# A written-out order for sigmoid attention with a token mixer: another order, eight casts on VectorE, no held transfers

## The chip, the cores and the metric

The kernel runs on one core of a Trainium2 chip. The metric is the device time of one execution in microseconds. A core has five engines with queues of their own, each worked off strictly in order: TensorE (PE; its weight loads are shown as PEld), VectorE (DVE), ScalarE (ACT), GpSimd (POOL) and SyncE (SP), which issues the transfers between HBM and the on-chip memory. A matmul writes to one of eight accumulator banks (PSUM), and VectorE or ScalarE has to copy it out before the bank is used again.

## The reference

For 8 batches, 12 heads, 448 tokens and a head size of 64, attention with a sigmoid in place of the softmax, and a token mixer on its output:

```python
scores = scale * np.matmul(q, k.transpose(0, 1, 3, 2)) - np.log(S)
attn = 1.0 / (1.0 + np.exp(-scores))
x = np.matmul(attn, v)                  # heads side by side: (8, 448, 768)
...
W_tok = scale * np.einsum('bsd,btd->bst', x @ w_q, x @ w_k)
mixed = np.einsum('bst,btd->bsd', W_tok, x)
out = np.maximum(mixed, 0.0) @ w_out
```

Inputs and output are float32. There is no normalisation in either part, so the mixer is reassociated: the kernel forms the 64 x 768 matrix of keys times x first, and multiplies the queries by it.

## The kernel before

**Units of work.** Four heads of a batch are a *quad*; there are 24 quads, three to a batch. A quad's scores come in seven pieces (168 in all). A piece is four 64 x 64 matmuls with 448 columns that run side by side on the four quarters of the array and fill a pair of banks; one sigmoid on ScalarE reads the pair and writes bf16 (line 332). Four more quarter-array matmuls multiply the piece with the values (`values`), and after seven pieces VectorE copies the quad's output to the tile `xt` (line 356).

**Steps of the mixer.** When a batch's three quads are there, the kernel transposes x (`tr_x`, copied out in line 385), projects it (`mlp_wqk`), transposes the keys, forms `tmp`, mixes (`mlp_mix`, relu in line 468 or 470) and multiplies by `w_out` (`out_chunk`, `out_pair`; copies in lines 604 and 651, stores in 612 and 657).

**Two tilings of the array.** Attention, `tmp` and the mix use quarters of the array (64*64 in the profile). The projection, the output product of the first four batches, and a part of the x transposes use the whole array (128*128). Every step from the one kind to the other is a change of tiling; there are 84 in the program. A few steps use 128*64.

**How q and k get into place.** q, k and v of a quad are loaded as float32 into a ring of six buffers (`ld`), cast to bf16 (line 212 for most q and k, line 222 for v and the first quads), and q and k are then turned so that the head dimension lies along the partitions. There are two ways for the later quads. Kind `c`: GpSimd swaps quadrants of the cast tile (`arrange`: one copy in line 167, two in 170, two in 173), and VectorE finishes with two 32 x 32 block transposes (line 272). Kind `r`: nothing on GpSimd, and VectorE makes six transposes (two in line 265, four in 252). The cast tiles have two buffers, so the casts for a quad wait until VectorE has read those of the quad two before.

**What sets the order.** Nothing is scheduled by a tool. `PLAN` is a string with one letter for each step: S a piece of scores with its sigmoid, T a piece of scores whose sigmoid is left to the next S, so that one ACTIVATE reads both, P and p a values product, q k the first quads' transposes, c and d the two transposes of a quad of kind `c`, r s z those of kind `r`, x y X Y the x transposes (capital: on the whole array), W w L l, N, U u, M m, O o the mixer's steps, D a store, C a copy of `w_out` to the other half of the partitions, E and F matmuls on zeros that keep TensorE busy at the start, 1 the next cast that VectorE does. Small letters of P, W, U, M and O put the copy out on ScalarE. `BANKS` gives each step its bank or pair of banks. `ORDER` is the order of loads and casts; an entry with a point in front is cast by VectorE, the others by GpSimd. A load is issued when the cast that frees its buffer has been written in the program. `BEHIND` makes two late loads wait for a given matmul, and `HELD` three stores.

Of the kernel before, what the change touches and what calls it, by code (L numbers as in the profile page):

```python
# [17 lines left out]
def kernel(  # L18
# [29 lines left out]
    def pool(name, bufs, **kw):  # L48
# [15 lines left out]
    pairs = [banks[:, 2 * n : 2 * n + 2] for n in range(4)]  # L64
    pairs16 = [banks16[:, 2 * n : 2 * n + 2] for n in range(4)]
    BANKS = (
        "abcd0123200233111020302312031203101031021g2012020120h1g21320"
        "132123103103213012302g01h20h1g2031a32102312g12h1201321gh0210"
        "12h01210321g201321g2h01gh201g20132cd302c302302131e301230ef31"
        "0ef3102102c302d320d320123cd20gh120g102310g102hg102312gh10210"  # L70
        "ef130210ef1302120120320312321031021021321a310320321320120123"
        "020210320120c3210210312"
    )
    given = list("".join(BANKS))
    held = set()
# [54 lines left out]
    def xt(u, j):  # L130
# [5 lines left out]


    PLAN = (
        "SSFKESSES1EEqESDD1DESjPPppSpDpPDSSSqS1kSpPPSqSpSkSDPPSPSxSxr"
        "sSWwDDDDSSwzDPpSPppSpPSrSwSwWsSPpXSPNpSpPPSUSqSzMSSkpSpPpSMS"  # L140
        "ppPSSxSxMScPpSdPSpppSSPwWwrWSSXWDWSSosOSNPpPSpppzPSSOOSxSrPP"
        "ppSUSsppzPSoSOSoSoSppMpSPPPPSSWOWWWScSdxWODSMDWSOSxCOSMppScP"
        "DppSPPDSodDoSpxPDPDSCPrPSpDSPOOSNSsSOoDzOOSUSXcSPdpPSSpPPSPo"
        "OWSMSwowWMSSOwWCScpppSxpdpSpPSOoMSPPcDSPPpSpSPOoNSSSdDOoDOOp"
        "xDSPpPxSPpPDSuwcWwdSSMWOoSMSDwwOOSDxpPSPrPSmPpPDooNDSDSosoOz"
        "oSDDSxOOSUDpSDPPPDSPpcDSPoDODSSSodOoOSPMpSPPPSPPSwWwoScMSdOw"
        "wSSWOONSPMPcpSPPPPSSOodXSOSxoSoxSOppSpcUPSPpPSoOSdSxOOSPPPmp"
        "pPSPoSoMmOSOLScllLSLLSDodODSONxOPSpcpdpDPSPSPoOSoSOSOoSUSoSO"
        "SpPPpp1SoSOpSPOSOyppPMpPpplMlmlxlLlxOoONooUoOMmooOmooOoOOOOO"
        "oOOOOooOo"  # L150
    )
    PLAN = "".join(PLAN)
    KIND = ["a"] + [t for t in PLAN if t in "qacr"]
# [364 lines left out]

    opened = []
    stores, o_tiles = [], [0]  # L520
    HELD = {(5, 1, 1): 3040, (5, 2, 0): 3168, (5, 2, 1): 3168}

    def flush(n=None):

# [45 lines left out]
    def out_pair(act, tail):  # L570
# [36 lines left out]
        def store():  # L607
            for x in range(2):
                cols = slice(x * NB, (x + 1) * NB)
                if len(us) == 1:  # L610
                    behind_product(
                        (nc.scalar if ends and x else nc.sync).dma_start(
                            out=out[2 * w + us[0]].rearrange("(p i) d -> p i d", i=NI)[:, k : k + 5 : 4, cols], in_=o[HALF[x]],
                        ), HELD.get((2 * w + us[0], k, x), 0),
                    )
# [6 lines left out]

        stores.append((o_tiles[0] - 1, max(HELD.get((2 * w + us[0], k, x), 0) for x in range(2)), store))
        if tail or late:
# [74 lines left out]
    for _ in range(31):  # L699
# [1 line left out]


    ORDER = (
# [5 lines left out]
    )  # L709
    BEHIND = {("q", 23): (2280, 2280), ("v", 23): (2816, 2530)}  # L710
    BY = {"s": [], "v": []}
    for x in ORDER.split():
        if x[0] == ".":
# [10 lines left out]
    def pump_loads():  # L724
        while len(loaded) < len(ORDER):
            nm, n = ORDER[len(loaded)]
            if len(ring) >= 6 and ring[-6] not in cast:
                break
            emit, m = BEHIND.get((nm, n), (0, 0))
            if emit >= len(products):  # L730
# [204 lines left out]
```

## Time and profile before

| | |
|---|---|
| times of 3 runs | 183.81, 184.26, 184.72 us; median 184.26 |
| profiled execution, its own time | 184.71 us |
| its span, first to last instruction | 182.8 us |
| granted TensorE clock, mean | 0.994 |
| busy: PE, PEld, DVE, ACT, POOL | 170.4, 112.8, 134.3, 159.4, 116.8 us |
| HBM read, written | 35.78 MB, 11.01 MB |

The span covers the instructions; 1.9 us of the profiled execution's time lie around it. A busy time is the time in which an engine has at least one instruction running. For TensorE it says little by itself, because its matmuls overlap: how fast it works is read from the starts of consecutive groups in the timeline. The timeline merges equal instructions of an engine that follow each other, gives their start and length, and in brackets the idle time before them with what ended it.

### The profile page before, as it was taken

Reading aid. Unit: us, or ns where it says so; the run is one execution under the profiler, and the core shown is the slowest. Engines: PE = TensorE matmul, PEld = TensorE weight load, DVE = VectorE, ACT = ScalarE, POOL = GpSimd, SP = SyncE. Lnnn points to the kernel's source line nnn. Section 1 sums busy time; section 2 is a strip of 40 time slices with the busy share of each in tenths; the row PEclk is TensorE's granted clock in tenths of the full one; section 3 lists DMA queues with packets and bytes.
Section 4 is the critical chain, followed back from the end, with each engine's and each line's share of the span. In section 5 each row is a group of like instructions: output and inputs, shape, how many; then the busy total and the mean of one; then the engine's idle time right before and its main releaser. Section 6 shows DMA issues by size and latency. Waiting matters only on the chain.

```text
span 182.8 us, 8404 instructions
## 1 busy us (share of the span) xinstructions
PE 170.4 (93%) x3617; PEld 112.8 (62%) x3618; DVE 134.3 (73%) x205; ACT 159.4 (87%) x207; POOL 116.8 (64%) x156
## 2 busy tenths in 40 slices
PE   7887789899999999999999999999999999999980
PEld 7644435545564555565556556556788798899960
DVE  2545699988998898988858887689786885694220
ACT  4699999999999999999998999899989979966230
POOL 1336886999589999699999927999999500000000
PEclk9999999999999999999999999999999999999997
DMA  5999999969999677999999999997589343433775
GB/s 174 371 382 274 329 382 398 364 212 279 351 402 331 219 295 207 353 285 349 396 232 327 349 307 292 359 359 250 193 255 252 106 96 87 95 90 93 176 181 164
DMA packets 24261, 48.51 MB, mean 265 GB/s; under 512 B 3872, under 2 KB 16416, under 8 KB 24224
## 3 DMA queue, kind: packets, MB, share of 16 engines
q1 hardware_dynamic: 24000, 47.69, 79.4%
q8 instruction: 28, 0.46, 1.0%
q10 hardware_dynamic: 224, 0.30, 0.7%
q14 instruction: 9, 0.07, 0.1%
HBM read 35.78 MB, written 11.01 MB: 256 GB/s over the span
## 4 chain that ended last, share of the span: by engine, by line
PE 76%; ACT 12%; DMA 3%; POOL 3%; issue 2%; DVE 1%; POOLq 0%; ACTq 0%
PE banks L121 72%; ACT at L332 12%; PE banks L124 4%; DMA ld<-in_v_dram 3%; POOL v L222 1%; POOL qk L212 1%; POOL qk L173 1%; POOL wout L755 0%; DVE xn L385 0%; ACT qk L806 0%; DVE ld L558 0%; ACT ld L558 0%; DVE zeros L691 0%; DVE zeros L690 0%; POOLq L222 0%
## 5 line engine op out<-in xcount | busy, mean ns | idle before, releaser
L332 ACT ACTIVATE at<-banks 128x896 bf16<-128x896 f32 x168 | 141.1, 943 | 5.4 <-PE banks L121 4.8
L121 PE MATMUL banks<-wout,mx 64*64 64x384 bf16 (+2 forms) x816 | 65.4, 324 | 0.0
L121 PE MATMUL banks<-qk 64*64 64x448 bf16 x672 | 60.7, 360 | 3.8 <-ACT at L332 3.0
L212 POOL CAST qk<-ld 128x896 bf16<-128x896 f32 x38 | 44.7, 1191 | 8.2 <-issue 5.6
L121 PEld LDWEIGHTS <-mx 64*64 64x64 bf16 (+2 forms) x816 | 39.2, 105 | 16.2 <-issue 6.0
L121 PE MATMUL banks<-at,v 64*64 64x448 bf16 x672 | 46.5, 350 | 0.8 <-ACT at L332 0.4
L121 PEld LDWEIGHTS <-qk 64*64 64x64 bf16 x672 | 26.5, 105 | 24.8 <-issue 17.8
L356 DVE CAST xt<-banks 128x896 bf16<-128x896 f32 x23 | 25.0, 1086 | 7.6 <-PE banks L121 5.7
L121 PEld LDWEIGHTS <-v 64*64 64x64 bf16 x672 | 22.9, 106 | 6.8 <-issue 1.7
L470 DVE TENSOR_SCALAR mx<-banks 128x896 bf16<-128x896 f32 (+1 forms) x21 | 19.9, 956 | 4.9 <-PE banks L121 4.2
L222 POOL CAST v<-ld 128x896 bf16<-128x896 f32 x22 | 20.3, 930 | 2.9 <-DMA ld<-in_v_dram 2.7
L272 DVE STREAM_TRANSPOSE qk<-qk 128x448 f32<-128x448 f32 x26 | 16.0, 630 | 0.1
L385 DVE COPY xn<-banks 128x896 bf16<-128x896 bf16 x21 | 13.1, 624 | 3.6 <-PE banks L124 2.6
L252 DVE STREAM_TRANSPOSE qk<-qk 32x448 f32<-32x448 f32 x24 | 15.3, 636 | 0.6
L170 POOL COPY qk<-qk 32x448 uint32<-32x448 uint32 x26 | 14.4, 554 | 1.6
L173 POOL COPY qk<-swap 32x448 uint32<-32x448 uint32 x26 | 14.4, 554 | 1.5
L121 PE MATMUL banks<-xt,wqk 64*64 64x448 bf16 (+1 forms) x84 | 13.8, 353 | 0.2 <-ACT at L332 0.2
L651 DVE COPY o<-banks 128x384 f32<-128x384 f32 x17 | 9.4, 554 | 3.4 <-PE banks L121 3.0
L124 PEld LDWEIGHTS <-xt 64*64 64x64 bf16 (+1 forms) x588 | 9.8, 108 | 3.0 <-issue 1.5
L124 PE MATMUL banks<-ident,xt 64*64 64x64 bf16 (+1 forms) x588 | 10.4, 194 | 0.2
L121 PE MATMUL banks<-wqk,tmp 64*64 64x448 bf16 (+3 forms) x72 | 8.5, 291 | 0.0
L121 PE MATMUL banks<-wq,tmp 64*64 64x448 bf16 (+2 forms) x72 | 8.4, 292 | 0.0
(67 smaller groups left out, 135.3 us busy)
## 6 DMA issues: line engine op xcount, KB each, us to landing
ld<-in_q_dram SPq DMA_DIRECT2D x24, 448.0 KB, 6.2
ld<-in_v_dram SPq DMA_DIRECT2D x24, 448.0 KB, 5.9
ld<-in_k_dram SPq DMA_DIRECT2D x23, 448.0 KB, 5.9
out_dram<-o SPq DMA_DIRECT2D x38, 192.0 KB, 4.7
out_dram<-ld SPq DMA_DIRECT2D x14, 192.0 KB, 2.8
ld<-in_moe_w_out_dram SPq DMA_DIRECT2D x6, 384.0 KB, 4.6
wout<-wout SPq DMA_DIRECT2D x6, 192.0 KB, 6.0
out_dram<-o SPq DMA_DIRECT2D x4, 96.0 KB, 1.9
```

What stands on the lines that cost most here:

```text
L121: products.append(nc.tensor.matmul(*args, **kw))
L124: products.append(nc.tensor.transpose(*args, **kw))
L170: eng.tensor_copy(out=w[lo, 1], in_=w[hi, 0])
L173: eng.tensor_copy(out=w[hi, 0], in_=z[lo])
L212: COPY[e](out=f[:, :, "qk".index(nm)].rearrange("p e i d y -> p e y i d"), in_=ld.pop((nm, n)).rearrange("p (y i e d) -> p e y i d", y=2, ...
L222: COPY[e](out=t16.rearrange("p i b d -> p b i d"), in_=ld.pop((nm, n)).rearrange("p b (i d) -> p b i d", i=NI),)
L252: nc.vector.transpose(out=qk[n][other : other + 32, h].rearrange("p t i n -> p (t i n)").bitcast(F32), in_=w[own : own + 32, 1 - h],)
L272: nc.vector.transpose(out=qk[n][:, t].rearrange("p t i n -> p (t i n)").bitcast(F32), in_=w)
L332: nc.scalar.activation(dst, src, ACTF.Sigmoid, bias=attn_bias, scale=attn_scale)
L356: COPY[eng](out=xt(u, j), in_=ps)
L385: COPY[eng](out=xn, in_=ps)
L470: nc.vector.tensor_scalar(dst, ps, moe_scale, 0.0, ALU.mult, ALU.max)
```

## The change

The order of all steps is another one. `PLAN`, `BANKS` and `ORDER` hold new strings, `BEHIND` and `HELD` are empty; no function is changed.

```diff
     BANKS = (
-        "abcd0123200233111020302312031203101031021g2012020120h1g21320"
+        "abcd23001212003333120321023102310331031231a2312321b3210g1301"
...
     PLAN = (
-        "SSFKESSES1EEqESDD1DESjPPppSpDpPDSSSqS1kSpPPSqSpSkSDPPSPSxSxr"
+        "SSFKESSESEEDDEqTSkSTS1DPpppppPSSqSkDDSPSDSPpDqkESPSpxPPSSSrx"
...
-    HELD = {(5, 1, 1): 3040, (5, 2, 0): 3168, (5, 2, 1): 3168}
+    HELD = {}
...
     ORDER = (
-        ".q1 k1 .v0 .k2 q2 v1 q3 k3 q4 w0 k4 v2 k5 q5 v3 q6 k6 v4 k7 w5 "
+        "q1 k1 v0 .k2 q2 v1 k3 q3 k4 q4 w0 v2 q5 k5 v3 q6 k6 k7 v4 w5 v6 "
...
-    BEHIND = {("q", 23): (2280, 2280), ("v", 23): (2816, 2530)}
+    BEHIND = {}
```

Counted in the built programs: 76 changes of tiling instead of 84; 164 sigmoids instead of 168, four of them over two pieces; 16 quads of kind `c` and three of kind `r` instead of 13 and six (quads 9, 12 and 17 went over); eight casts on VectorE after the first quad instead of four (k2, v5, k11, v11, q16, v18, v21, v23; before q1, v0, k2, v23); one x transpose more on the whole array, five instead of four; VectorE copies three output halves of line 651 less and three output pairs of line 604 more, ScalarE three more and three less.

ScalarE at the start, in the order of its instructions; each row is a line, the operation, out<-in and the size:

```order
 L806 COPY qk<-banks 128x3x2x64
-L332 ACTIVATE at<-banks 128x896 x63
+L332 ACTIVATE at<-banks 128x896 x5
+L332 ACTIVATE at<-banks 128x1792
+L332 ACTIVATE at<-banks 128x896
+L332 ACTIVATE at<-banks 128x1792
+L332 ACTIVATE at<-banks 128x896 x53
 L651 COPY o<-banks 128x384
```

The first 63 pieces of scores go through 61 sigmoids: pieces 6 and 7, and 9 and 10, are taken together.

GpSimd around quad 9, whose cast tile is qk_1133 before and qk_1144 now (`swap` is the scratch tile of `arrange`, `wq` the copy of the projected queries, `wout` the cast of `w_out`):

```order
-L222 CAST v_978<-ld_101 128x2x7x64
-L222 CAST v_981<-ld_102 128x2x7x64
-L212 CAST qk_1133<-ld_103 128x2x2x224
-L212 CAST qk_1133<-ld_104 128x2x2x224
+L755 CAST wout_83<-ld_101 128x768
+L222 CAST v_1010<-ld_102 128x2x7x64
+L212 CAST qk_1144<-ld_103 128x2x2x224
+L212 CAST qk_1144<-ld_104 128x2x2x224
+L167 COPY swap<-qk_1144 128x448
+L170 COPY qk_1144<-qk_1144 32x448 x2
+L173 COPY qk_1144<-swap 32x448 x2
 L438 COPY wq_99<-wqk_97 64x448
```

Quad 9 is now of kind `c`: five quadrant copies stand between its casts and everything that GpSimd does afterwards.

VectorE at the same place (qk_1275 before and qk_1250 now are quad 10, qk_1418 is quad 11):

```order
-L265 STREAM_TRANSPOSE qk<-qk_1133 128x448 x2
+L272 STREAM_TRANSPOSE qk<-qk_1144 128x448
 L463 CAST tmp<-banks 128x384
-L252 STREAM_TRANSPOSE qk<-qk_1133 32x448 x4
+L272 STREAM_TRANSPOSE qk<-qk_1144 128x448
 L356 CAST xt_91<-banks 128x2x7x64
 L651 COPY o<-banks 128x384
+L212 CAST qk_1418<-ld_102 128x2x2x224
 L470 TENSOR_SCALAR mx<-banks 128x2x448
+L272 STREAM_TRANSPOSE qk<-qk_1250 128x448
 L356 CAST xt_92<-banks 128x2x7x64
-L272 STREAM_TRANSPOSE qk<-qk_1275 128x448 x2
```

Six transposes of quad 9 became two, a cast of quad 11 moved in, and the first transpose of quad 10 stands ahead of a copy of xt that it stood behind.

More of the change, by code (lines that the diff above doesn't have):

```diff
@@ L66 @@
     BANKS = (
-        "abcd0123200233111020302312031203101031021g2012020120h1g21320"
[L68 to L72, printed above, removed]
+        "abcd23001212003333120321023102310331031231a2312321b3210g1301"
+        "302132130130123021302g01h20h1g2031a32102312h1021g01301gh0210"
+        "12h01210321g201321g2h01gh201320132cd302c302302131e031203e01f"
+        "3ef1032102c320d302d320103cd02gh120g021302g021hg021302gh10210"
+        "ef130213fe1302120120320312321031021021321a310320321320120123"
+        "020120320cd3a0203103210"
     )
@@ L138 @@
     PLAN = (
-        "SSFKESSES1EEqESDD1DESjPPppSpDpPDSSSqS1kSpPPSqSpSkSDPPSPSxSxr"
[L140 to L150, printed above, removed]
+        "SSFKESSESEEDDEqTSkSTS1DPpppppPSSqSkDDSPSDSPpDqkESPSpxPPSSSrx"
+        "SWSSpPPPPSspzPSWwWSSrwWXSPsSpPPSNPPPSUSSSqzMDSkSppDPSPS1MpDS"
+        "PPSxSxSMSPPcPSDPdpSPPSwrwDwWSSXwWSSsOOSDNzppSpPPpSSPoOSxSPpp"
+        "PScDUSDdPpPSoSODSpSOoSp1McPSppCpSPSDWdWoWSSxOWWMSSODWSxOSDMD"
+        "pPScPppDSPPdSODDoSPpxSpPpPSSPOOSNcSDS1ooCdOOSUSxScPppSPPSpSd"
+        "POOWSMSWwOWMSDSWWOSpPpcSxPPSpPSodoSMcPPSDpppSPPSOOSSdN1SoDOO"
+        "oxCSDppxPpSPpPSUcWWwwSSMoWodSSMWOoSpxDPScPPPDpSDPmOodNSSOOoT"
+        "SxoOoSUPSPpPcSPPPSDo1oDSTSocOOodSMppSPpPpdSPSwDWWoSMSOwWSDDS"
+        "WooNSMPpSppcDpPdSPSXooScoSxOSOxSOpdPPPSUSppPSDOSoSxOOcSpmDPp"
+        "PPpSPoSOM1moSOlSlLdLSlLSoocSoNxOPpSPSPPPSPooSOSOdSoOSUSOS1OS"
+        "PPPpPSpOSPoSoSOpPxPpmPppMllDLmLlDlXXOoNoOuOOMODmOMOoOOoOOOOo"
+        "ooOoooOoOo"
     )
```

8 rows, old and new, of the table ORDER are left out of this document.

## The prediction

> **What bounds the kernel now.** I read the table of stages first: busy time of each engine, granted clock, share of the transfer engines.
>
> ```profile
> 10.00:20.00 10.00, 7.88 (x244) 4.54 (x244) 4.76 (x7) 9.77 (x14) 5.52 (x7) 1.00 0.96 311
> 20.00:30.00 10.00, 8.63 (x161) 4.24 (x156) 9.38 (x15) 10.00 (x14) 8.51 (x10) 1.00 1.03 383
> ...
> 50.00:60.00 10.00, 10.00 (x182) 5.52 (x178) 9.17 (x14) 9.98 (x14) 8.75 (x12) 1.00 1.00 366
> 60.00:100.00 40.00, 40.00 (x727) 22.77 (x720) 34.03 (x50) 38.40 (x50) 36.72 (x48) 1.00 0.90 295
> 100.00:140.00 40.00, 40.00 (x784) 25.53 (x788) 31.44 (x49) 37.90 (x50) 33.89 (x46) 1.00 0.87 291
> 140.00:160.00 20.00, 20.00 (x542) 17.46 (x537) 14.59 (x21) 18.91 (x24) 4.13 (x7) 1.00 0.43 111
> ```
>
> The columns are stage, its length, then busy time of PE, PEld, DVE, ACT, POOL. From 10 to 60 us ScalarE is hardly ever idle while TensorE has gaps; from 50 us on TensorE has none. So two engines take turns, and the table shows where: ScalarE paces to somewhere between 50 and 60 us, TensorE afterwards. The chain of waits says the same, TensorE's own work with ScalarE in front of it:
>
> ```profile
> PE 76%; ACT 12%; DMA 3%; POOL 3%; issue 2%; DVE 1%; POOLq 0%; ACTq 0%
> ```
>
> The timeline of ScalarE gives its pace, that of VectorE the end:
>
> ```profile
> 6.71 5.78 ACT L332 ACTIVATE at<-banks 128x896 bf16<-128x896 f32 x7 [0.69 <-PE banks L121]
> 12.72 46.07 ACT L332 ACTIVATE at<-banks 128x896 bf16<-128x896 f32 x56 [0.23 <-PE banks L121]
> ...
> 177.62 0.36 DVE L558 COPY ld<-banks 128x192 f32<-128x192 f32 x1 [0.56 <-PE banks L121]
> ```
>
> 63 sigmoids (nine quads) run from 6.71 to 58.79 us with one gap of 0.23 us. In the long row one starts every (46.07 - 0.94) / 55 = 0.82 us, since a sigmoid of 0.943 us (row below) overlaps the next. TensorE ends just before 177.6 us, and a copy and a store fill the rest to 182.8 us.
>
> The time is therefore the start, plus 63 paces of ScalarE, plus TensorE's work behind them, plus the last store. A term counts if it shortens one of these.
>
> **The change, part by part. Changes of tiling.** Starts of consecutive groups in TensorE's timeline:
>
> ```profile
> 45.27 0.56 PE L124 MATMUL banks<-ident,xt 128*128 128x128 bf16 x7
> 45.67 0.54 PE L121 MATMUL banks<-xt,wqk 128*128 128x448 bf16 x2
> ...
> 57.69 0.66 PE L121 MATMUL banks<-wout,mx 128*128 128x384 bf16 x3
> 58.28 0.38 PE L121 MATMUL banks<-qk 64*64 64x448 bf16 x4
> ...
> 84.39 0.66 PE L121 MATMUL banks<-wout,mx 128*128 128x384 bf16 x3
> 84.88 0.54 PE L121 MATMUL banks<-xt,wqk 128*128 128x448 bf16 x2
> ...
> 86.33 0.39 PE L124 MATMUL banks<-ident,xt 64*64 64x64 bf16 x28
> 86.54 0.55 PE L121 MATMUL banks<-at,v 64*64 64x448 bf16 x8
> 86.92 0.37 PE L121 MATMUL banks<-qk 64*64 64x448 bf16 x4
> ```
>
> Three output products take 0.59 us when quarters follow (57.69 to 58.28) and 0.49 when whole-array work follows (84.39 to 84.88): a change costs 0.10 us, and eight fewer save 0.8. One x transpose on the whole array (45.27 to 45.67, 0.40) in place of quarters (86.33 to 86.54, 0.21) gives 0.19 back: 0.6 in all. But six of the eight lie in front of the 64th piece of scores, where TensorE waits for ScalarE anyway: counted in the two orders, 55 changes are left there before and 53 now. That is 2 x 0.10 saved, less 0.19 for the third x transpose on the whole array that now lies there instead of two, and one values product fewer is left (111 for 112; two groups from 86.54 to 86.92, so 0.19). Sum on the path: **-0.2 us**. The other end: from the 99th piece on, 31 changes are left for 29 and two more x transposes on the whole array, +0.2 and +0.4, and if ScalarE still paced until there, this would be what counts. Range -0.6 to +0.6.
>
> **Sigmoids over two pieces.** Rows of ScalarE and of the casts and transposes below:
>
> ```profile
> L332 ACT ACTIVATE at<-banks 128x896 bf16<-128x896 f32 x168 | 141.1, 943 | 5.4 <-PE banks L121 4.8
> L468 ACT ACTIVATE mx<-banks 128x448 bf16<-128x448 f32 x6 | 3.1, 545 | 1.7 <-PE banks L121 1.7
> L468 ACT ACTIVATE mx<-banks 128x896 bf16<-128x896 f32 x3 | 2.8, 928 | 0.0
> L212 POOL CAST qk<-ld 128x896 bf16<-128x896 f32 x38 | 44.7, 1191 | 8.2 <-issue 5.6 <-DMA ld<-in_k_dram 1.0 <-DMA ld<-in_q_dram 0.9
> L222 POOL CAST v<-ld 128x896 bf16<-128x896 f32 x22 | 20.3, 930 | 2.9 <-DMA ld<-in_v_dram 2.7
> L222 DVE CAST v<-ld 128x896 bf16<-128x896 f32 x2 | 1.2, 618 | 0.0
> L272 DVE STREAM_TRANSPOSE qk<-qk 128x448 f32<-128x448 f32 x26 | 16.0, 630 | 0.1
> L252 DVE STREAM_TRANSPOSE qk<-qk 32x448 f32<-32x448 f32 x24 | 15.3, 636 | 0.6
> L170 POOL COPY qk<-qk 32x448 uint32<-32x448 uint32 x26 | 14.4, 554 | 1.6
> ```
>
> The trace has no ACTIVATE of 1792. Two relu rows give (928 - 545) / 448 = 0.855 ns an element, so 896 elements are 0.766 us of the pace of 0.82, and a joined pair saves the remaining 0.05; by full lengths it would be 943 - 766 = 0.18. Two pairs lie in front: **-0.1 us**, range 0 to -0.35.
>
> **The gap at 12.72 us.** ScalarE waited there for the eighth piece, the first of quad 1. Before, the k transposes of quad 1 (letter j, one copy for q and k together) stand behind piece 7; now they are a k with two smaller copies, and ScalarE has the joined pieces 6 and 7 to work on meanwhile. **-0.2 us**. The range goes from -0.23 to +0.8: a joined sigmoid holds two of the four pairs of banks, and should the next piece find none, ScalarE loses a pace.
>
> **VectorE and ScalarE.** Three quads of kind r that became c take four transposes each from VectorE, 12 x 0.636 = 7.6 us. Four more casts come in: two of line 222 at 0.618; two of line 212, which VectorE has not run, between 0.618 (its row for the same bytes) and 1.191 (GpSimd's for the same form), and I take 0.8, since GpSimd pays 1191 / 930 for that form. With these VectorE does 7.6 - 1.2 - 1.6 = 4.8 us less. It was idle for 6 of the 40 us from 60 to 100, so nothing of it is on the path: 0, and what it hides behind is TensorE's full row. ScalarE's exchanged copies lie in the same stage: 0.
>
> **GpSimd.** It takes on 3 x 5 quadrant copies, 15 x 0.554 = 8.3 us, and loses two casts of each line, 2 x (1.191 + 0.930) = 4.2: about +4.1 us on an engine that had 3.3 us free from 60 to 100. Its queue is strict, and so is VectorE's: a first transpose that stands ahead of GpSimd's last copy blocks every copy out of the banks behind it. The places:
>
> ```profile
> 47.42 0.93 POOL L222 CAST v<-ld 128x896 bf16<-128x896 f32 x1 [1.51 <-DMA ld<-in_v_dram]
> ...
> 56.77 0.56 POOL L167 COPY swap<-qk 128x448 uint32<-128x448 uint32 x1
> 57.39 1.17 POOL L170 COPY qk<-qk 32x448 uint32<-32x448 uint32 x2
> 58.62 1.17 POOL L173 COPY qk<-swap 32x448 uint32<-32x448 uint32 x2
> 59.85 1.20 POOL L212 CAST qk<-ld 128x896 bf16<-128x896 f32 x1
> ...
> 88.92 1.17 POOL L173 COPY qk<-swap 32x448 uint32<-32x448 uint32 x2
> ```
>
> ```profile
> 59.49 1.09 DVE L470 TENSOR_SCALAR mx<-banks 128x896 bf16<-128x896 f32 x1 [0.47 <-PE banks L121]
> 60.56 1.09 DVE L356 CAST xt<-banks 128x896 bf16<-128x896 f32 x1
> 61.68 1.17 DVE L272 STREAM_TRANSPOSE qk<-qk 128x448 f32<-128x448 f32 x2
> ...
> 90.39 0.64 DVE L272 STREAM_TRANSPOSE qk<-qk 128x448 f32<-128x448 f32 x1
> ```
>
> Quad 10 was arranged at 59.8 us and transposed at 61.7. Now quad 9's five copies (56.77 to 59.85, 3.1 us) come ahead and one v cast (0.9) has moved away: 62.0, or 60.5 if the wait of 1.51 us for a load at 47.42 is gone. VectorE comes to it right after the mix copy, at about 60.6: up to 1.4 us late. Quad 15 was arranged at 90.1 and transposed at 90.4, so there was no slack; quad 12's copies add 2.8, the casts of k11 and v11 leave with 2.1, so it inherits the lateness of quad 10 and 0.7. Behind the transposes stands the copy of xt, whose banks TensorE needs two or three pieces later; those pieces hide most of 1.4 us. **+0.1 us**, range 0 to +2.8.
>
> **No transfer held, and the end.** The last loads have long landed when they are needed, and the transfer engines are busy for 0.43 of 140 to 160 us: 0. After the last mix 20 steps of the output product follow instead of 18, so the last copies stay covered: 0.
>
> **Sum:** -0.2 - 0.1 - 0.2 + 0.1 = -0.4 us. The profiled execution took 184.71 us, 0.45 above the median; it would take 184.3, and the median goes from 184.26 to **183.9 us**. A measurement can tell about 0.5%, 0.92 us, from no change: 183.34 to 185.18.
>
> **Rivals.** *Faster:* the front is not pure waiting, and TensorE, with lighter VectorE and ScalarE, keeps all it is given: the whole 0.6, the pairs at 0.35, the gap at 0.23, -1.2 us: 183.1. For it speaks that VectorE was busy 9.38 of 10 us from 20 to 30, so its copies came late; against it that ScalarE had no gap there.
>
> *Slower:* GpSimd becomes the clock. If quad 10 is arranged after about 61 us, quads 10 and 15 each hold VectorE for 1.4 us; two pieces hide 0.8 of it together, and the gains of 0.5 go against it: 2.8 - 0.8 - 0.5 = +1.5, 185.8. For it speak the 36.72 busy us of 40 and the 0.3 us of slack at 90.4; against it that VectorE has less to do and catches up. The casts on VectorE may add to it, which no run here shows, since the four of before start at 7.9, 10.1, 14.4 and 155.4 us, at most 0.1 us beside GpSimd work. [...]
>
> *The front breaks:* a joined sigmoid costs a pace, +0.8 instead of -0.2: 184.9.
>
> **Chances.** Forecast 0.43 (own range 183.3 to 184.6), faster rival 0.27, slower 0.22, broken front 0.08. Of the forecast 0.08 lies below 183.34 and 0.02 above 185.18, of the faster rival 0.05 lies within, of the slower 0.02, of the front 0.02 above: faster 0.30, same 0.46, slower 0.24. The range is 182.6 to 186.0.
>
> **What the new profile would show.** Right: sigmoids without a gap to about 58.5 us; TensorE full from 55 us; the same 5 us from TensorE's end to the span's. Starts 0.10 us apart at each change. Wrong: waits of a VectorE transpose in line 272 for GpSimd near 61 and 91 us, with TensorE waiting for banks after them; or waits for an xt or mx copy before 60 us; or a joined sigmoid that starts behind a gap.

## The result, and the profile after

The changed kernel takes **186.44 us** (186.16 to 186.97) where the kernel before takes 184.26: a ratio of 1.0105, 95% interval 1.0066 to 1.0144. The forecast was 183.9 in a range of 182.6 to 186.0; it is slower by 1%, and above the range. Ratios here and below leave disturbed executions out; a median of all executions stands beside them. The profiled execution of the change took 186.97 us with a span of 185.1; that of before took 184.71 with 182.8. So 2.3 us are to be found between the two spans.

The table of stages of the changed kernel (stage, length, busy time of PE, PEld, DVE, ACT, POOL, granted clock, DMA share, GB/s):

```profile
10.00:20.00 10.00, 6.75 (x221) 4.12 (x221) 4.85 (x6) 9.81 (x11) 6.44 (x7) 1.00 1.09 363
20.00:30.00 10.00, 7.18 (x151) 4.01 (x151) 6.98 (x11) 7.94 (x10) 8.49 (x11) 1.00 1.01 356
50.00:60.00 10.00, 9.90 (x194) 5.69 (x189) 8.75 (x14) 9.97 (x13) 9.45 (x13) 1.00 0.88 319
60.00:100.00 40.00, 39.80 (x748) 22.70 (x749) 31.95 (x47) 38.57 (x50) 37.62 (x52) 1.00 0.89 289
100.00:140.00 40.00, 40.00 (x787) 24.99 (x779) 29.08 (x44) 37.72 (x50) 36.27 (x51) 1.00 0.90 302
140.00:160.00 20.00, 20.00 (x518) 17.39 (x510) 14.40 (x20) 18.95 (x24) 5.78 (x8) 1.00 0.45 117
```

Everything behind 50 us looks as before. The loss stands in one row: from 20 to 30 us ScalarE was busy for 7.94 us where it had been busy for 10.00, with TensorE at 7.18 for 8.63. One stage ahead of it the DMA share is 1.09 where it was 0.96. The timelines of ScalarE and, for the end, of VectorE in the changed kernel:

```profile
6.71 13.10 ACT L332 ACTIVATE at<-banks 128x896 bf16<-128x896 f32 x14 [0.69 <-PE banks L121]
22.06 38.58 ACT L332 ACTIVATE at<-banks 128x896 bf16<-128x896 f32 x47 [2.25 <-PE banks L121]
...
179.69 0.36 DVE L558 COPY ld<-banks 128x192 f32<-128x192 f32 x1 [0.62 <-PE banks L121]
```

The gap of 0.23 us at 12.72 is gone, as forecast, and a gap of 2.25 us at 19.8 us has come that no part of the forecast has. ScalarE waited for TensorE; TensorE's own timeline, and that of its weight loads, say for what:

```profile
18.29 0.39 PE L124 MATMUL banks<-ident,q 64*64 64x64 bf16 x28
18.51 0.40 PE L124 MATMUL banks<-ident,k 64*64 64x64 bf16 x28
19.05 0.35 PE L121 MATMUL banks<-zeros 64*64 64x448 bf16 x1
21.39 0.38 PE L121 MATMUL banks<-zeros 64*64 64x448 bf16 x3 [1.99 <-issue]
21.40 0.56 PE L121 MATMUL banks<-qk 64*64 64x448 bf16 x4
...
19.05 0.10 PEld L121 LDWEIGHTS <-zeros 64*64 64x64 bf16 x1 [0.24 <-issue]
21.39 0.10 PEld L121 LDWEIGHTS <-zeros 64*64 64x64 bf16 x2 [2.23 <-issue]
```

This is the reading to learn: TensorE stood for over 2 us **between the first and the second of four matmuls of one step**, which all write one pair of banks and read only zeros. Nothing between them can wait for another engine, and the profile names no releaser: "issue" is time in which the engine waited for nothing that it shows. (The bracket of a matmul, 1.99, starts at a modelled end. Here and below a gap is counted from the start of the last weight load ahead of it to that of the next: 19.05 to 21.39, 2.34 us.) What is left that it could have lacked, besides data and banks, is instructions. The profile's transfer queues have one of the kind "instruction", q8, with 28 packets of 16 KB. The views of transfers, over two stretches of the kernel before (14.6 to 15.6 us, then 15.6 to 15.8; queue: packets, MB, share of 16 engines):

```profile
q1 hardware_dynamic: 136, 0.37, 96.0%
...
q8 instruction: 1, 0.02, 43.8%
q1 hardware_dynamic: 14, 0.03, 39.9%
```

and over two of the changed kernel (15.3 to 18.6 us, then 18.6 to 18.7):

```profile
q1 hardware_dynamic: 1595, 1.11, 113.8%
...
q1 hardware_dynamic: 46, 0.02, 111.4%
q8 instruction: 1, 0.02, 82.2%
```

In both kernels the engines were full of loads while the packet waited; before, the loads had run down to 40% when it started, 1.1 us after it was asked for. In the change it still ran beside a full queue, and started after 3.4 us. How these two times come about can be counted. TensorE's stream has 7,193 recorded rows (3,597 weight loads and 3,596 matmuls), so 28 packets make some 256 rows a packet. The rows of the changed kernel at the place, counted from the program's first weight load (number, line, instruction):

```
701 L121 LDWEIGHTS zeros
702 L121 MATMUL banks<-zeros 64x448
703 L121 LDWEIGHTS zeros
704 L121 MATMUL banks<-zeros 64x448
705 L121 LDWEIGHTS zeros
```

TensorE stopped behind row 703, and 704 is 192 + 2 x 256. In both profiled kernels each of the 28 packets starts -0.2 to 6.3 us after TensorE reaches the last weight load ahead of a row 192 + 256k (in the longest, 2.3 us of it are the gap at row 704 itself). And each but the last ends 1.4 to 6.8 us ahead of the first row behind the next such border. I read these times so, since the asking itself stands in no trace: a packet is the block of 256 rows behind the next border, and the time of asking, here and below, is when TensorE reaches the last weight load ahead of a border. By this reading a block has to last as long as the next one takes to come:

```
                      asked  loads under  packet      rows ready   256 rows   TensorE
block at row 704      at us  way then     starts/ends (+1.4 us)    lasted us  stood
kernel before         14.59      3        15.68 17.08    18.5        4.30     no
changed kernel        15.28      6        18.67 19.99    21.39       3.77     2.3 us
```

The 1.4 us from a packet's end to its use is what the changed kernel's gap shows (19.99 to 21.39); for the kernel before it is an estimate from there. By it the block was ready 0.4 us ahead of its use. The change moved the loads forward (k of quad 4 and both small weight loads are now issued by 14.0 us; before, q of quad 4 at 10.74 was followed only at 15.02), so six loads were under way when the block was asked for, not three, and its packet started 2.3 us later after the asking. And it put the transposes of q and k of quad 3, 112 rows in 0.6 us, back to back, so the rows ran out 0.5 us earlier.

Where the sigmoids stand says that this is nearly the whole of it (end of the nth score piece's sigmoid in us, from the traces):

```
piece        7     14     21     28     63     98    140    168   last copy  span
before    12.48  18.49  24.16  29.84  58.79  90.48 132.50 159.20   178.33   182.8
change    12.58  18.19  26.22  31.90  60.64  92.35 134.08 160.90   180.41   185.1
change -  +0.10  -0.30  +2.06  +2.06  +1.85  +1.87  +1.58  +1.70    +2.08    +2.3
```

Up to the 14th piece the change gains 0.3 us, as forecast; between the 14th and the 21st it loses 2.36; from there to the last copy only tenths change hands.

### The profile page after: what moved, and what is told of

Its sections match the earlier page's. It is cut to its first block, busy times and chain, and to the rows that moved or that the text cites. A ratio compares the mean times of both kernels' runs of the same rounds, so it can differ in the third digit from the quotient of the medians.

```text
span 185.1 us, 8361 instructions
## 1 busy us (share of the span) xinstructions
PE 169.5 (92%) x3596; PEld 112.8 (61%) x3597; DVE 129.9 (70%) x197; ACT 157.6 (85%) x201; POOL 123.8 (67%) x168
## 4 chain that ended last, share of the span: by engine, by line
PE 73%; ACT 16%; DVE 4%; issue 3%; ACTq 0%; DVEq 0%
PE banks L121 69%; ACT at L332 16%; PE banks L124 4%; DVE xn L385 1%; DVE xt L356 1%; DVE qk L301 1%; DVE mx L470 1%; DVE qk L272 0%; ACT qk L806 0%; ACT o L651 0%; DVE ld L558 0%; ACT ld L558 0%; DVE zeros L691 0%; ACTq L332 0%; DVE zeros L690 0%
## 5 line engine op out<-in xcount | busy, mean ns | idle before, releaser
L332 ACT ACTIVATE at<-banks 128x896 bf16<-128x896 f32 (+1 forms) x164 | 140.6, 957 | 7.7 <-PE banks L121 6.3
L212 POOL CAST qk<-ld 128x896 bf16<-128x896 f32 x36 | 42.5, 1205 | 3.5 <-DVE qk L272 1.2
L272 DVE STREAM_TRANSPOSE qk<-qk 128x448 f32<-128x448 f32 x32 | 20.0, 632 | 1.0 <-POOL qk L173 0.9
L173 POOL COPY qk<-swap 32x448 uint32<-32x448 uint32 x32 | 18.7, 584 | 1.9
L170 POOL COPY qk<-qk 32x448 uint32<-32x448 uint32 x32 | 18.5, 578 | 1.9
L222 POOL CAST v<-ld 128x896 bf16<-128x896 f32 x19 | 17.7, 931 | 2.1 <-DMA ld<-in_v_dram 1.2
L121 PE MATMUL banks<-xt,wqk 64*64 64x448 bf16 (+1 forms) x84 | 13.2, 352 | 0.1
L124 PEld LDWEIGHTS <-xt 64*64 64x64 bf16 (+1 forms) x567 | 9.7, 108 | 3.1 <-issue 1.3
L124 PE MATMUL banks<-ident,xt 64*64 64x64 bf16 (+1 forms) x567 | 10.5, 195 | 0.0
L167 POOL COPY swap<-qk 128x448 uint32<-128x448 uint32 x16 | 9.0, 561 | 0.9
L651 DVE COPY o<-banks 128x384 f32<-128x384 f32 x14 | 7.7, 554 | 2.6 <-PE banks L121 2.5
L121 PE MATMUL banks<-zeros 128*128 128x132 bf16 (+1 forms) x55 | 5.8, 332 | 3.5 <-issue 2.0
```

Of the source, the lines that this page charges most:

```text
L121: products.append(nc.tensor.matmul(*args, **kw))
L124: products.append(nc.tensor.transpose(*args, **kw))
L167: eng.tensor_copy(out=z, in_=w[:, 1])
L170: eng.tensor_copy(out=w[lo, 1], in_=w[hi, 0])
L173: eng.tensor_copy(out=w[hi, 0], in_=z[lo])
L212: COPY[e](out=f[:, :, "qk".index(nm)].rearrange("p e i d y -> p e y i d"), in_=ld.pop((nm, n)).rearrange("p (y i e d) -> p e y i d", y=2, ...
```

## The experiments

All are told with the ratio to the kernel before, which was timed beside them on the same chip.

**The filler alone.** The matmuls on zeros in which TensorE stood are left out (step E behind "qk" of quad 3, and its bank's letter):

```diff
-...SPDSPpDqkESPSpxPPSSSrx
+...SPDSPpDqkSPSpxPPSSSrx
```

> The changed kernel without its sixth filler (the four matmuls on zeros at 19 us, inside which TensorE stood for 2.0 us). Theory (instruction supply): TensorE's instructions come in blocks of 256, each by one 16 KB packet of the instruction queue that is asked for when TensorE enters the block before; block 704 to 959 was asked for at 15.28 us, its packet started 3.39 us later behind loads, ended at 19.99, and TensorE had used up the 256 rows before it in 3.77 us. Without the filler's 8 rows the same block is late just the same: a gap of 2.0 to 2.6 us stays at row 704, now inside the scores that follow, and the time stays at 186.4 us (186.0 to 186.9). Rival (the filler waits for its bank pair, which a sigmoid has to release): the gap goes with the filler, about 184.2 us.

Measured: 186.64 us, ratio 1.0089 (1.0053 to 1.0124). TensorE's timeline of this run:

```profile
18.08 0.40 PE L124 MATMUL banks<-ident,k 64*64 64x64 bf16 x28
18.62 0.35 PE L121 MATMUL banks<-qk 64*64 64x448 bf16 x1
20.88 0.46 PE L121 MATMUL banks<-qk 64*64 64x448 bf16 x3 [1.91 <-issue]
```

The filler is gone and the gap stays, 2.26 us between rows 703 and 704, now in the middle of a score piece. It belongs to the row's number and not to the filler, and the rival of a filler that waits for its banks falls.

**The same work, 112 rows later.** 64 tiny matmuls ahead of the warm-up, 8 of the 31 warm-up matmuls less:

```diff
-    for _ in range(31):
+    for _ in range(16):
+        for g in range(2):
+            for h in range(2):
+                mm(pairs[3][HALF[h], g, 0:8], zeros[HALF[g], 0:NP], zeros[HALF[g], 0:8], start=True, stop=True)
+    for _ in range(23):
```

> The changed kernel with 64 tiny matmuls on zeros (64x64 tiles, 8 columns) ahead of the warm-up and 8 of the 31 warm-up matmuls left out: 112 rows more ahead of everything on TensorE, the same work after it. Theory (blocks of 256 rows): the block borders move 112 rows towards the start of the work: the border that stood in the filler at 19.05 us now stands in the transposes of quad 3's q near 18.2 us, and the 256 rows before it last 6.5 us, so no gap there; the next border stands 144 rows behind the filler, the 256 rows before it last some 4.4 us while a block needs about 6 us from the asking, so a gap of 1 to 2 us opens there; time 185.7 us (184.8 to 186.5). Rival (the place in the work makes the gap, not the number of the row): the gap stays inside the filler with 2.0 us, 186.4 us.

The timeline of TensorE in this run:

```profile
18.85 0.38 PE L121 MATMUL banks<-zeros 64*64 64x448 bf16 x4
...
22.38 0.22 PE L124 MATMUL banks<-ident,xt 64*64 64x64 bf16 x5
23.73 0.38 PE L124 MATMUL banks<-ident,xt 64*64 64x64 bf16 x23 [1.12 <-issue]
```

The filler's four matmuls now run in one piece, and a gap of 1.32 us stands some 140 rows behind them, at row 960, in the middle of 28 transposes. Place and size are as expected (1 to 2 us). The time is not: a median of 188.72 us, ratio 1.0143 (1.0072 to 1.0214), where 185.7 was expected. The trace shows why. The borders further back moved too, and three more blocks came late, at rows 2752, 5056 and 5312: 1.52, 0.58 and 1.64 us at 72.8, 136.9 and 141.7 us. I had looked at the front alone. (The profiled execution took 188.76 us, and the six lie between 185.95 and 190.28; how many of these late blocks the quicker ones had is not shown.)

**Traffic put into the kernel before.** Two loads more, into tiles that nobody reads:

```diff
             loaded.add((nm, n))
+            if (nm, n) == ("q", 4):
+                for y in range(2):
+                    nc.sync.dma_start(out=spare[y]..., in_=SRC["v"][7, 4 * y : 4 * y + 4]...)
```

> The kernel before, with two loads more of 448 KB into tiles that nobody reads, issued right behind q of quad 4 on SyncE's queue (near 11 us). Its TensorE stream is the same row for row. There the packet of block 704 was asked for at 14.59 us, started 1.09 us later in a thin stretch of traffic, and arrived 0.4 us ahead of its use. Theory: the added traffic fills that stretch, the packet starts 2.5 to 4 us after the asking, and a gap of 1 to 2.4 us that no semaphore explains opens at row 704 (near 18.9 us) in a kernel that had none; time 186.0 us (185.2 to 187.2). Rival (traffic doesn't delay instructions): no such gap; the loads behind, w0 and k of quad 4, land up to 2.5 us later, which costs 0 to 1 us at most, 184.3 to 185.2 us.

Measured: 187.19 us, ratio 1.0123 (1.0084 to 1.0161). TensorE, whose rows are those of the kernel before one by one (the edit shifts the lines by one, L125 is L124):

```profile
18.82 0.35 PE L125 MATMUL banks<-ident,k 64*64 64x64 bf16 x21
20.32 0.25 PE L125 MATMUL banks<-ident,k 64*64 64x64 bf16 x7 [1.15 <-issue]
```

Five loads were under way when block 704 was asked for, its packet started 3.07 us later instead of 1.09, and a gap of 1.34 us opened at row 704 of a kernel that had none. This isolates the cause: no row moved, and only loads of bytes that nobody uses were put in. (The time lost is larger than the gap; the loads behind the spare ones landed up to 3.1 us later, so this run doesn't price the gap.)

**One load held.** q of quad 4 behind a matmul, near 15.5 us, and in a second run near 13.4 (it was issued at 17.12 and 14.19 us in the two profiles, at 12.26 in the changed kernel):

```diff
-    BEHIND = {}
+    BEHIND = {("q", 4): (228, 226)}      # second run: (200, 190)
```

> The changed kernel with one load held: q of quad 4 (issued at 12.26 us) waits for matmul 226, about 15.5 us, and w0 and what follows it on SyncE's queue with it. No row of TensorE's stream moves. Theory (instruction supply, late because the DMA engines are full): at 15.3 us the queue is nearly empty as it was in the kernel before (where the packet started 1.09 us after it was asked for), the packet starts within 1.6 us instead of 3.39, the gap at row 704 is under 0.5 us, and the time is 184.4 us (183.9 to 185.0). Rival (supply is late for a reason that the loads don't set, or the gap has another cause): gap and time stay, 186.4 us or more. Third possibility: the held load is itself late and ScalarE starves at quad 4, over 187 us.

> As the run with q of quad 4 held, but behind matmul 190 (13.4 us) in place of 226 (15.5), so that the load lands near 19.4 us as it did unheld (12.26 us issued, 19.36 landed) and nothing behind it comes much later. Theory (a packet waits for the loads that are under way when it is asked for: with 3 under way it started 0.8 and 1.1 us after the asking, with 5 or 6 3.1 to 3.4): at 15.28 us 3 or 4 are under way, the packet starts 1 to 2.5 us after the asking, the gap at row 704 is 0 to 1.3 us instead of 2.3, time 185.0 us (184.3 to 185.8), under the 186.1 of the longer hold. Rival (the gap follows the row alone, and the longer hold gained by something else): gap 2.3 us, 186.4 us.

The long hold: ratio 1.0052 (1.0019 to 1.0084), median 186.12. Three loads under way, the packet started 0.79 us after the asking, TensorE found its rows. The mechanism did what was expected, the time only half. Why is open: in the profiled execution, 189.56 us long, v of quad 2 was in at 26.63 us instead of 22.15, but loads were late before the hold could act (q of quad 2 landed at 15.15 us, 12.50 in the changed kernel), the granted clock was 0.50 from 8.5 to 11.9 us, and a late block took 0.67 us at row 5312. That the hold gives late rows back and takes late data fits this, and is not shown by it. The short hold: packet 2.31 us after the asking, the gap 1.30 us, inside the expected 0 to 1.3; but six loads were under way, not three or four, and the median is 186.55, ratio 1.0103 (1.0069 to 1.0136), no gain that can be told from the change's 1.0105. Holding a load is no cheap cure here.

**Fewer rows for the same work.** Transposes of quads 2 and 3 on the whole array, 7 matmuls for 28, in the changed kernel and, as a control, in the kernel before (letters a and b for q and k; their banks in `BANKS` change too, not shown):

```diff
-...SSqSkDDSPSDSPpDqkES...
+...SSaSbDDSPSDSPpDabES...
```

> The changed kernel with the transposes of q and k of quads 2 and 3 on the whole array (7 matmuls each where 28 on 64x64 tiles stood): the same work on 168 rows fewer, of which 84 lie ahead of row 704. Loads and queues as in the changed kernel. Theory (instruction supply): the 256 rows ahead of row 704 now reach to 22.7 us of the changed kernel's clock and last about 6.9 us, where the block needs about 6.1 from the asking (3.4 to its packet's start, 1.3 for it, 1.4 until it is used), so no gap over 0.4 us in TensorE up to 40 us that no semaphore explains; the whole-array transposes take 0.8 us in place of 0.4 on a TensorE that waits for ScalarE there, which may cost up to 0.4; time 184.4 us (183.9 to 185.1). Rival (traffic of the loads itself starves the front, and the gap only shows it): gaps of the same sum elsewhere in the front, 186.4 us.

> The kernel before with the same whole-array transposes for quads 2 and 3, a control. There the block at row 704 came 0.4 us ahead of its use, so there is no gap to close. Theory: no gain from instruction supply, 184.4 us (184.0 to 185.0). Rival (whole-array transposes are better by themselves in the front): 183.0 to 183.8, and then what the changed kernel gains by them is no evidence on the gap.

ScalarE of the changed kernel with this edit:

```profile
6.67 52.02 ACT L332 ACTIVATE at<-banks 128x896 bf16<-128x896 f32 x61 [0.65 <-PE banks L121]
```

One row from 6.67 to 58.69 us without a gap: the 63rd piece ends at 58.70 us, 1.94 earlier than in the changed kernel and 0.09 earlier than before. But the time is 186.03 us, ratio 1.0083 (1.0043 to 1.0123). The 168 rows less moved every border behind, and TensorE shows what that cost:

```profile
72.04 0.35 PE L121 MATMUL banks<-qk 64*64 64x448 bf16 x3
72.66 0.54 PE L121 MATMUL banks<-qk 64*64 64x448 bf16 x5 [0.27 <-issue]
```

0.80 us between the starts of two weight loads at row 2496, and 0.39 and 0.30 at rows 4800 and 5056. The expectation of 184.4 looked at the front alone, as with the shift. The control took 185.37, ratio 1.0040 (1.0014 to 1.0066), where 184.4 was expected: whole-array transposes are no gain by themselves, rather a loss.

**Rows put back behind the front.** 84 tiny matmuls, three ahead of each score piece of quads 3 to 6:

```diff
+        for x in range(3 if 3 <= n <= 6 else 0):
+            mm(sc[HALF[x % 2], x // 2, 0:8], zeros[HALF[x // 2], 0:NP], zeros[HALF[x // 2], 0:8], start=True, stop=True)
```

> The run with whole-array transposes in quads 2 and 3, and the 168 rows that they took out put back behind row 704 as 84 tiny matmuls on zeros (64x64 tiles, 8 columns), three ahead of each score piece of quads 3 to 6, where TensorE waits for ScalarE; from quad 7 on every row has the number that it has in the changed kernel. The run without the padding closed the gap of the front, but its later block borders stood elsewhere and 0.80 us went at 71.9 us, 0.47 at 100, 0.39 at 135 and 0.30 at 140, where rows were used 0.6 to 1.6 us behind their packet's end. Theory (where a border falls decides): no gap that no semaphore explains at row 704 nor at these four places over 0.25 us; the 63rd score piece ends near 58.8 us instead of 60.6, time 184.7 us (184.2 to 185.4). Rival (the later gaps came from the different pace of the front, not from the borders): they stay, and the time with them at 185.5 to 186.3 us.

None of the border gaps of the last run is left, and from the 63rd to the 168th piece this run needs 100.23 us, the changed kernel 100.26: the gaps there came from the borders. (The 0.47 at 100 us that the expectation names stood at a border, row 3520, but was no late block: the same step of 0.47 us, from the weights of `tmp` to those of `mx`, stands in the changed kernel at 101.92 us, where no border is. I had put it down wrongly.) But the padding made the rows of 30 to 40 us dense, and blocks 1216 and 1472 came late (the lines show the second; L334 is L332 of the other runs):

```profile
39.51 0.20 PE L121 MATMUL banks<-zeros 64*64 64x8 bf16 x2 [0.18 <-ACT at L334]
40.47 0.16 PE L121 MATMUL banks<-zeros 64*64 64x8 bf16 x1 [0.77 <-issue]
```

0.45 and 0.96 us, and 187.33 us in all, ratio 1.0113 (1.0069 to 1.0157), where 184.7 was expected. A miss in time that repeats the cause at two new places.

**Rows taken out ahead of the front instead**, 82 of them, with the whole-array transposes in the changed kernel, and alone in the kernel before:

```diff
-    for _ in range(31):
-        mm(pairs[3][:, 0, 0 : 132], zeros[:, 0:P], zeros[:, 0 : 132], start=True, stop=True)
+    for _ in range(8):
+        mm(pairs[3][:, 0], zeros[:, 0:P], zeros, start=True, stop=True)
     # and in PLAN every E (four matmuls on quarters) as F (one on the whole array)
```

> The run with whole-array transposes in quads 2 and 3, and in place of the padding 82 rows fewer ahead of everything: the 31 warm-up matmuls over 132 columns as 8 over 512 (the same columns), the six fillers of four matmuls as one matmul over 512 columns each. With the 168 rows that the transposes save, TensorE has 250 rows fewer, almost one block, so from quad 4 on the borders stand within 6 rows of where they stand in the changed kernel, and no rows are added where the padding opened new gaps (0.45 and 0.96 us at 34 and 39 us). Theory: in the front each 256 rows last 6.5 us or more against the 5.9 to 6.1 that a block took there, so no gap over 0.3 us that no semaphore explains anywhere; the 63rd score piece ends near 58.6 us (60.6 in the changed kernel), time 184.4 us (183.9 to 185.3), 2 us under the changed kernel and level with the kernel before. Rival (what the changed order gains or loses has further causes in the front): 185.5 us or more.

> The kernel before with the same saving of 82 rows in warm-up and fillers, nothing else: it computes the same with fewer instructions. Theory (where a border falls decides): the second border moves from where the score pieces and transposes of quad 2 gave 4.3 us with thin traffic to a stretch asked for at 10.9 us, with 5 or 6 loads under way, whose 256 rows last 4.3 us against 5.5 to 6 that the block needs: a gap of 1 to 1.6 us opens near 15.2 us, and 185.8 us (185.0 to 186.8) against 184.4 of the kernel before. Rival (fewer instructions can only help): 184.4 us or less, no such gap.

The changed kernel so edited, ScalarE and then TensorE:

```profile
12.30 7.33 ACT L332 ACTIVATE at<-banks 128x896 bf16<-128x896 f32 x8 [0.18 <-PE banks L121]
19.96 38.89 ACT L332 ACTIVATE at<-banks 128x896 bf16<-128x896 f32 x47 [0.32 <-PE banks L121]
...
136.37 0.23 PE L124 MATMUL banks<-ident,xt 64*64 64x64 bf16 x5
137.11 0.38 PE L124 MATMUL banks<-ident,xt 64*64 64x64 bf16 x23 [0.51 <-issue]
```

The gap of 2.25 us at 19.8 is 0.32; the 63rd piece ends at 58.85 us (expected 58.6), the 140th at 132.37, 1.71 ahead of the changed kernel and 0.13 ahead of the kernel before. Then one block at row 4800 came late by 0.71 us: its packet took 2.31 us where that of the changed kernel's block took 1.05. The median is 185.84 us, ratio 1.0068 (1.0034 to 1.0102), for an expected 184.4: 0.6 us under the changed kernel, its interval overlapping the other's. In the kernel before, 82 rows fewer gave 185.19 us, ratio 1.0046 (1.0016 to 1.0075): slower with fewer instructions, though by less than expected. The gap expected at 15.2 us is not in the profiled execution (the packet came 2.42 us after the asking, just in time), which took 184.20 us, near the fastest; so the loss of the other executions has no line that shows it; a gap of 0.31 us at row 1984 is all that the profile has.

**The joined sigmoids.** Four T as S (two of them shown):

```diff
-"SSFKESSESEEDDEqTSkSTS1D..."
+"SSFKESSESEEDDEqSSkSSS1D..."
```

> The changed kernel with its four sigmoids over two score pieces split into eight over one: ScalarE's four extra starts come back, TensorE's rows stay where they are. By the prediction's term for the joined sigmoids (-0.1 us, 0 to -0.35): 186.5 us (186.2 to 186.9), gap at row 704 2.0 to 2.5 us as before. Rival (the joined sigmoids hold two bank pairs at once and so made the front late): 185 us or less and the gap smaller.

Measured: 187.21 us, ratio 1.0152 (1.0115 to 1.0188), 0.8 us above the change, so over the expected range: the joined sigmoids may be worth more than the forecast's 0.1, though the profiled executions, 186.94 and 186.97 us, don't show it. The 14th piece ends at 18.49 us instead of 18.19. The gap at row 704 is there, 1.49 us, so they did not make it.

Over all runs the gaps at a border can be told by their signature alone. In eleven of the thirteen profiles 17 gaps of 0.3 to 2.3 us stand exactly behind a row 191 + 256k, in transposes, score pieces and fillers alike, and in all 17 TensorE goes on 1.3 to 1.5 us after a 16 KB packet has ended. Both marks are needed, because steps of 0.3 us between two weight loads are common (some hundred a profile): three more at a border, of 0.4 to 0.5 us, come 2.1 to 4.9 us after their packets and are not counted. By another mark: behind 8 us each idle time of TensorE of 0.15 us and more that a profile puts down to "issue", 13 in all, stands at a border. Three of the 17, by the run: 2.34 us, 1.40 behind (the change, row 704); 1.64 us, 1.46 behind (112 rows later, row 5312); 0.96 us, 1.32 behind (padded, row 1472).

## Why the prediction was wrong

**The step that failed** is the one on loads: "No transfer held, and the end: ... 0". It asked only whether the last loads land in time, found that they do, and wrote 0; the new order of the early loads has no term in the sum. What they collide with in the front was never asked, and there the change lost 2.36 us. The row to see it by was in the first fence: a DMA share of 0.96 at 311 GB/s from 10 to 20 us, with some room left. The order of loads shows that w0, one load further back now, no longer waits for VectorE's cast of k2, which has also moved from 14.37 us to 11.62; that fills the room, and what it pushes back is the instruction packet. The prediction had "the front breaks" as a rival at +0.8 for a joined sigmoid that finds no banks, 0.08 of the chances. The front broke, by something else, at nearly three times the price.

A second premise fell with it: "TensorE waits for ScalarE anyway" in the front, so that what TensorE does there costs nothing. TensorE has time to spare there on average (8.63 busy of 10.00), and still stood for want of rows, since 256 rows with two quads' transposes in quarters went in 3.8 us.

The size of the blocks could have been read from the kernel before: its page has `q8 instruction: 28, 0.46, 1.0%`, and its trace 7,235 rows of TensorE. The thirteen profiles agree: 27 packets in the three with 6,944 to 7,067 rows, 28 in the ten with 7,154 to 7,306, and the 28th border is at row 7,104. In the changed kernel the block at row 704 took 6.1 us from the asking to its use, and the 256 rows before it lasted 3.77; that left 2.3 us. What turned it into a cost is the traffic: the packet started 3.39 us after the asking with six loads under way, and 1.09 with three in the kernel before.

**The other terms**, by the profiled executions:

- Joined sigmoids and the gap at 12.72, -0.1 and -0.2: at the 14th piece the change is 0.30 ahead. Right to a tenth. The form that the trace of before lacked now has its row (below): 1678 ns for two pieces against two of 939, so 0.825 ns an element more, where 0.855 was worked out. Their price may be too low all the same: undone, the time rose by 0.8, though the two intervals overlap.
- Tiling on the path, -0.2 (-0.6 to +0.6): from the 63rd piece to the last copy before needs 119.54 us and the change 119.77, so +0.2; inside the range, other sign. Which part of the remainder gave it was not told apart.
- GpSimd, +0.1 of a possible +2.8, and the rival that makes it the clock: VectorE's transposes of line 272 waited 0.9 us for it in all, at two places, and ScalarE's pieces 63 to 98 took 31.71 us where they took 31.69. Right that nobody waits; the work was under-costed, 123.8 us busy for 116.8, +7.0 and not +4.1. What the prediction left open, that VectorE's casts may add to it, the runs show. A cast of this size takes VectorE 0.62 to 0.63 us where GpSimd is idle. Beside GpSimd's work it took 0.58 to 1.59 us, and the two of line 212 took 0.76 and 0.96 in the change and 1.16 and 1.10 without the joined sigmoids, so that 0.8 came near is luck. In the change six GpSimd instructions beside VectorE's casts took 0.28 to 0.44 us more than their like, 2.15 of the missing 2.9 us; in all thirteen profiles each GpSimd cast of 896 columns and each quadrant copy that took over 0.1 us more than its like ran beside such a cast.
- The end: from the last copy to the span's end 4.7 us, 4.5 before. Right.

The groups of the changed kernel behind these (line, engine, operation, tiles, count; busy us, mean ns; idle time ahead and its releaser), shapes kept apart:

```profile
L332 ACT ACTIVATE at<-banks 128x896 bf16<-128x896 f32 x160 | 134.6, 939 | 7.3 <-PE banks L121 5.8 <-DVE o L604 0.6
L212 POOL CAST qk<-ld 128x896 bf16<-128x896 f32 x36 | 42.5, 1205 | 3.5 <-DVE qk L272 1.2 <-DMA ld<-in_q_dram 1.2 <-DMA ld<-in_k_dram 0.3
L272 DVE STREAM_TRANSPOSE qk<-qk 128x448 f32<-128x448 f32 x32 | 20.0, 632 | 1.0 <-POOL qk L173 0.9
L332 ACT ACTIVATE at<-banks 128x1792 bf16<-128x1792 f32 x4 | 6.7, 1678 | 0.5 <-PE banks L121 0.5
```

and the two casts of line 212 on VectorE, with the GpSimd cast that ran beside the second (its like take 1.19 us):

```profile
59.02 0.76 DVE L212 CAST qk<-ld 128x896 bf16<-128x896 f32 x1
...
95.83 0.96 DVE L212 CAST qk<-ld 128x896 bf16<-128x896 f32 x1
...
96.20 1.63 POOL L212 CAST qk<-ld 128x896 bf16<-128x896 f32 x1
```

**What stays open.** That the gap at row 704 comes from a late block is shown: it keeps its row when the step there is taken out, moves with the count of rows, and appears in the kernel before when only traffic is added. That the changed kernel without it would be level with the kernel before is shown in one profiled execution up to the 140th piece, not in a median: each edit that closed the gap moved other borders, and no version here beats both kernels.

## What to carry to other kernels

When TensorE stands with "issue" as the releaser, in the middle of instructions that wait for nothing, look whether it stands at a border (here row 192 + 256k, as all 13 such times of 0.15 us and more behind 8 us did), and when that block's packet ran. Where small matmuls come in crowds while loads fill the transfer engines, spread them, do them with fewer instructions, or let the loads start a little later (the best two edits here brought the ratio from 1.0105 to 1.0052 and 1.0068, with intervals that overlap the change's); and count the rows of the whole stream, since taking out or adding any ahead moves every border behind. In forecasting a new order, ask of an earlier transfer not only whether it lands in time but what it pushes back.

## What the runs showed of the hardware

**How long an instruction packet waits.** Over the 13 profiles, 28 or 27 packets each, by the number of loads and stores under way when the block is asked for, the median time until its packet starts:

```
under way   0-2    3     4     5     6     7     8
packets     101   48    57    85    44    20     6
median us   0.7   1.1   2.0   2.3   3.0   2.6   2.1
```

The longest wait was 6.26 us, with six; it holds the gap of 2.34 us at row 704 of the changed kernel, and from that gap's end it was 3.9. The table shows that it waits longer the more there are, up to six: a median of 0.7 us with two or fewer and of 3.0 with six. What ranks the packet among the loads was not tried.

**A gap may cost twice.** Windows of the run without the filler, around its gap (stage, length, busy times, then granted clock, DMA share, GB/s):

```profile
20.00:21.00 1.00, 0.12 (x4) 0.12 (x7) 0.00 (x0) 0.00 (x0) 0.37 (x2) 1.00 1.06 401
21.00:22.00 1.00, 1.00 (x17) 0.70 (x16) 0.00 (x0) 0.56 (x1) 0.88 (x3) 0.53 1.01 398
22.00:23.00 1.00, 1.00 (x41) 0.97 (x36) 0.12 (x1) 1.00 (x2) 0.92 (x2) 0.50 1.00 382
23.00:24.00 1.00, 1.00 (x16) 0.71 (x8) 0.88 (x2) 0.17 (x1) 0.98 (x2) 0.50 1.06 385
24.00:25.00 1.00, 0.56 (x8) 0.11 (x4) 1.00 (x2) 0.94 (x2) 1.00 (x1) 0.77 1.07 378
```

Behind a gap of 2.3 us TensorE was granted half its clock for some 3.4 us; in the changed kernel, behind one of the same length, it kept the whole. In the run with 112 rows more the clock was 0.50 near 26 to 28 us, some 2 us behind its gap of 1.32. A late block is not needed for it: in the control with whole-array transposes in the kernel before, the clock was 0.50 from 8.1 to 11.5 us, behind a wait of 1.34 us for VectorE:

```profile
7.89 0.58 PE L124 MATMUL banks<-ident,k 64*64 64x64 bf16 x16 [1.34 <-DVE k L816]
...
9.00:10.00 1.00, 1.00 (x16) 0.55 (x14) 0.35 (x1) 0.72 (x1) 0.06 (x1) 0.50 1.03 396
```

So the same gap has more than one price, which fits the wide spread of the runs with such gaps (185.2 to 187.3 us without the filler); that the gap brings the fall is not shown. The stands ahead of the three falls told here were of 2.26, 1.32 and 1.34 us.
